# One fixed order of 966 operations exchanged for another, in a kernel of a state-space convolution and a gated MLP

## The chip, the core and the metric

The kernel runs on one core of a Trainium2 chip. The core has five engines with queues of their own: TensorE (PE in the profile; PEld is its weight load), VectorE (DVE), ScalarE (ACT), GpSimd (POOL) and SyncE (SP), which here only issues DMAs. An engine works off its queue in order. The metric is the device time of one launch in microseconds (us), lower is better.

## The reference

The input `u` (1 x 2048 x 512) is normalised along its last axis. The result is the sum of the input, a diagonal state-space convolution (S4) of the normalised rows, and a gated MLP (512 to 1792 and back) of them. Cut to what is computed:

```python
xn = layernorm(x)
# S4: kernel K from 128 modes for each of the 512 channels, then a causal convolution by FFT
dt = exp(log_dt)[:, None]
P = exp((dt * A)[:, :, None] * arange(2048)[None, None, :])
K = einsum("dn,dnl,dn->dl", C, P, dt * B).real
y = irfft(rfft(pad(xn)) * rfft(pad(K)))[:L] + xn * Dskip
# gated MLP
h = (sigmoid(xn @ w_gate) * (xn @ w_up)) @ w_down
return x + y + h
```

## The kernel before

The kernel builds a list of 966 operations with `_Plan.add`. Each has an engine, the operations that it depends on, and the buffers that it takes and gives back. The number of an operation in this list is its entry number below. `_Plan.run` goes through the hand-fixed list `ORDER` and emits the operations in exactly that order. Since an engine works off its queue in order, `ORDER` fixes the queue of each of the five engines. It also decides which buffer of a pool an operation gets: `run` takes the one that has been free longest. The framework puts a semaphore wait wherever an operation needs the result of another engine, or a buffer that another engine still reads. The plan's own costs play no part once `ORDER` is given.

The stages overlap. They are, in rough order of time:

- **Head, to about 16 us.** The first rows of x are loaded and normalised, TensorE is kept busy by warm-up products (L521), and the first gate products run.
- **Gated MLP.** The 2048 rows are four groups of 512. For each group there are 14 gate products (`fg`, L1036) and 14 up products (`fu`, L1060), each of four 128x128 by 512 matmuls. ScalarE takes the sigmoid (L1048, or L1051 for two at once), the up product is either copied by ScalarE (`feu`, L1072) or read from PSUM by VectorE, and VectorE multiplies (`fpd`, L1076). Four down products (`fd`, L1105, 14 matmuls each) end a group.
- **Kernel of the convolution.** ScalarE and VectorE build powers of the modes (L662 to L677, then L735 to L795 in four blocks), TensorE sums over the modes (L820).
- **Forward transform.** `fx2` (L694) transforms pairs of 128 rows, ScalarE or VectorE evicts them, and 16 stores write them to `z_scr` in HBM. All 16 must have landed before the first reload from it.
- **Units.** Twice eight units of half the channels each: a reload from `z_scr`, products `fm` (L882), an eviction, a swap of partition quarters (by DMA `big<-big` in the first half, by VectorE in the second), products with a table `c_E` (`fk`, L904), two VectorE multiplications (L909, L913), products back (`fv`, L926), an eviction and a store to `v_scr`.
- **Tail.** `reload()` reads `v_scr` back in three parts (entries 843 to 846, 847 to 850, 851 to 854), and the last products (`s2_mm`, L985) add the convolution to the MLP's results, beside the down products of the last group. Sums go out by DMA.

Products use different tile modes of TensorE: the large ones the whole array, `fm` and `fv` quarters of it, and others again halves or strips.

PSUM is 8 banks: two pairs (pool `s`) and four single banks (pool `gu`), so a product must wait until an earlier result has been read out of its bank.

Nearly all DMAs are issued by SP, in its order, some by ACT and POOL. A DMA that waits for data holds up all those behind it in SP's queue.

Of the kernel before, what the change touches and what calls it, by code (L numbers as in the profile page):

```python
# [178 lines left out]
def _consts():  # L179
# [20 lines left out]
ON_DVE = (88, 91, 106, 108, 123, 124, 125, 139, 140, 186, 196, 197, 200, 201, 203,)  # L200
ON_ACT = (2,)
ORDER = [
# [43 lines left out]

class _Op:
    __slots__ = ("alt", "tab", "eng", "cost", "fn", "prio", "acq", "rel", "dma", "left", "users", "ready", "start", "done", "seq", "mode")
# [946 lines left out]
```

## Time and profile before

| | |
|---|---|
| time of three runs | 218.53, 219.88, 219.86 us (median 219.86) |
| span of the profiled execution, first to last instruction | 217.6 us |
| TensorE busy | 209.0 us (96%), 1876 matmuls |
| VectorE busy | 193.8 us (89%) |
| ScalarE busy | 179.5 us (83%) |
| granted TensorE clock | 1.000 |
| moved by DMA | 42.80 MB |

The profile is of one execution. The page gives its span alone; the times of the runs are those of whole executions, and their median is 2.3 us above the span. A TensorE that counts as busy may still be in the pipeline of its matmuls, so its idle time is read from what it waited for. The helper that issues DMAs is one line (L421) and so is the copy by ScalarE (L287); they are told apart by the tiles that they write and read.

### The profile page before, as it was taken

To read this page: it belongs to the slowest core of one execution; us is meant where nothing else is said; L and a number is where in the kernel's file an instruction comes from. 1 tells how busy PE (TensorE), PEld (TensorE's weight loads), DVE (VectorE), ACT (ScalarE), POOL (GpSimd) and SP (SyncE) were. 2 spreads that over 40 slices of the span, in tenths; PEclk is the share of its full clock that TensorE was granted. 3 is DMA by queue.
4 is the path that set the end of the run, shared out by engine and by line. 5 is a ranking of instruction groups with operands and counts; after the bars stand their busy time and mean duration, and the time that the engine had idled before them with its cause. 6 is when DMAs were issued, how large, how long until landed. Compare 5 with 4: busy or idle time off the path is not lost.

```text
span 217.6 us, 4946 instructions
## 1 busy us (share of the span) xinstructions
PE 209.0 (96%) x1876; PEld 104.0 (48%) x1876; DVE 193.8 (89%) x438; ACT 179.5 (83%) x286; POOL 18.8 (9%) x40
## 2 busy tenths in 40 slices
PE   7979999999999999989999999999999999999894
PEld 2435444444444454435455565445546556544463
DVE  3989999999999999999999999999999999970433
ACT  3799999999999999869989999976897999960111
POOL 1410202002100020012000002010800000000000
PEclk9999999999999999999999999999999999999999
DMA  6999936001463689865697679929959969984974
GB/s 186 316 369 390 299 116 146 0 3 48 145 156 97 233 249 156 264 143 105 166 271 202 183 224 209 239 79 216 216 116 252 282 188 263 267 245 139 269 256 166
DMA packets 51530, 42.80 MB, mean 197 GB/s; under 512 B 16434, under 2 KB 43571, under 8 KB 51507
## 3 DMA queue, kind: packets, MB, share of 16 engines
q1 hardware_dynamic: 50338, 40.60, 63.8%
q0 software_dynamic: 864, 1.57, 5.5%
q10 hardware_dynamic: 304, 0.33, 0.6%
q8 instruction: 14, 0.23, 0.4%
q14 instruction: 10, 0.07, 0.1%
HBM read 25.97 MB, written 12.85 MB: 178 GB/s over the span
## 4 chain that ended last, share of the span: by engine, by line
PE 64%; DMA 17%; ACT 8%; SPq 7%; issue 2%; DVE 0%; ACTq 0%
PE bank L1060 18%; PE bank L1036 16%; PE bank L1105 10%; PE pair L904 7%; SPq L421 7%; DMA wu_sb<-in_B_w_up_dram 5%; PE pair L926 4%; ACT big L287 4%; DMA z_scr<-big 3%; DMA big<-big 3%; DMA big<-z_scr 2%; DMA v_scr<-big 2%; PE pair L882 2%; PE pair L820 2%; ACT us_sb L1072 2%
## 5 line engine op out<-in xcount | busy, mean ns | idle before, releaser
L287 ACT ACTIVATE big<-pair 128x1024 bf16<-128x1024 f32 x64 | 66.2, 1060 | 4.9 <-PE pair L926 1.5
L1060 PE MATMUL bank<-xnT,wu_sb 128*128 128x512 bf16 x224 | 54.5, 380 | 0.5 <-DMA wu_sb<-in_B_w_up_dram 0.4
L1036 PE MATMUL bank<-xnT,wg_sb 128*128 128x512 bf16 (+1 forms) x220 | 50.7, 368 | 1.9 <-DMA wg_sb<-in_B_w_gate_dram 1.8
L1105 PE MATMUL bank<-wd_sb,hT_sb 128*128 128x512 bf16 (+1 forms) x238 | 50.4, 367 | 0.0
L1036 PEld LDWEIGHTS <-wg_sb 128*128 128x128 bf16 x236 | 22.2, 98 | 26.9 <-issue 2.5
L1105 PEld LDWEIGHTS <-hT_sb 128*128 128x128 bf16 x238 | 22.6, 98 | 25.2 <-issue 1.9
L1060 PEld LDWEIGHTS <-wu_sb 128*128 128x128 bf16 x224 | 20.6, 98 | 25.2 <-issue 3.0
L1048 ACT ACTIVATE hT_sb<-bank 128x512 bf16<-128x512 f32 x52 | 30.9, 636 | 1.2 <-PE bank L1036 1.1
L735 DVE TENSOR_TENSOR big<-big 128x1024 bf16<-128x1024 bf16 (+4 forms) x40 | 26.8, 670 | 0.3 <-ACT big L287 0.2
L736 DVE TENSOR_TENSOR big<-big 128x1024 bf16<-128x1024 bf16 (+4 forms) x40 | 26.7, 667 | 0.0
L1072 ACT ACTIVATE us_sb<-bank 128x512 bf16<-128x512 f32 x40 | 25.9, 648 | 0.3
L909 DVE TENSOR_TENSOR big<-big 128x2048 bf16<-128x2048 bf16 x16 | 19.5, 1218 | 0.6 <-PE pair L926 0.3
L904 PE MATMUL pair<-big 128*128 128x256 bf16 x160 | 19.8, 273 | 0.0
L789 ACT ACTIVATE sq_sb<-big 128x256 bf16<-128x256 bf16 (+2 forms) x20 | 13.8, 691 | 5.1 <-DVE big L741 4.9
L904 PEld LDWEIGHTS <-big 128*128 128x128 bf16 x160 | 15.4, 98 | 4.9 <-issue 1.0
L1076 DVE TENSOR_TENSOR hT_sb<-hT_sb,us_sb 128x512 bf16<-128x512 bf16 x40 | 16.5, 418 | 0.4 <-ACT us_sb L1072 0.3
L740 DVE TENSOR_TENSOR big<-big 128x512 bf16<-128x512 bf16 (+4 forms) x40 | 16.5, 414 | 0.1
L741 DVE TENSOR_TENSOR big<-big 128x512 bf16<-128x512 bf16 (+4 forms) x40 | 16.5, 413 | 0.0
L1007 ACT ACTIVATE big<-pair 128x1024 bf16<-128x1024 f32 x3 | 3.1, 1023 | 15.2 <-PE pair L985 12.4
L895 DVE COPY big<-big 32x1024 bf16<-32x1024 bf16 x32 | 13.4, 419 | 0.6
L1011 DVE TENSOR_TENSOR big<-pair,glu_sb 128x1024 bf16<-128x1024 f32 x2 | 2.5, 1226 | 11.7 <-PE pair L985 8.1
L541 DVE BATCH_NORM_STATS2 stats<-big 128x6 f32<-128x512 bf16 x15 | 9.8, 682 | 3.4 <-DMA big<-in_A_u_dram 3.4
(104 smaller groups left out, 244.3 us busy)
## 6 DMA issues: line engine op xcount, KB each, us to landing
big<-c_E SPq DMA_DIRECT2D x16, 320.0 KB, 3.9
z_scr<-big SPq DMA_DIRECT2D x16, 256.0 KB, 2.9
big<-z_scr SPq DMA_DIRECT2D x16, 256.0 KB, 4.9
v_scr<-big SPq DMA_DIRECT2D x16, 256.0 KB, 3.1
big<-in_A_u_dram SPq DMA_DIRECT2D x4, 512.0 KB, 8.2
big<-big SPq DMA_DIRECT2D x32, 64.0 KB, 3.6
wu_sb<-in_B_w_up_dram SPq DMA_DIRECT2D x2, 896.0 KB, 10.7
wd_sb<-in_B_w_down_dram SPq DMA_DIRECT2D x1, 1792.0 KB, 15.1
```

Source lines behind the costliest of these rows:

```text
L287: nc.scalar.activation(out=get(out), in_=get(in_), func=ACT.Identity)
L735: V.tensor_tensor(out=wide(outp), in0=wide(lo), in1=mre, op=ALU.mult)
L736: V.tensor_tensor(out=wide(tb()), in0=wide(lo), in1=mim, op=ALU.mult)
L740: V.tensor_tensor(out=outp[:, :, 0], in0=outp[:, :, 0], in1=tb()[:, :, 1], op=opr)
L741: V.tensor_tensor(out=outp[:, :, 1], in0=outp[:, :, 1], in1=tb()[:, :, 0], op=opi)
L904: T.matmul(two(sk)[:, o:o + DW], es()[:, g, kt, :], kTv[p][:, :, kt, :], start=kt in (0, NKT - 1), stop=kt >= NKT - 2)
L909: V.tensor_tensor(out=pp().rearrange("p q h m -> p (q h) m"), in0=xx().rearrange("p q h m -> p (q h) m"), in1=kb()[:, 0:2 * DW].unsqueeze( ...
L1036: T.matmul(bank(sl, k % 2)[:, c0:c1], w[:, kt, k * 128:(k + 1) * 128], xnT[:, grp, kt, c0:c1], start=(kt == 0), stop=(kt == KT - 1))
L1048: S.activation(out=hT_sb[:, hs.idx, k % 2, :], in_=bank(sl), func=ACT.Sigmoid)
L1060: T.matmul(bank(sl), wu_sb[:, kt, k * 128:(k + 1) * 128], xnT[:, grp, kt, :], start=(kt == 0), stop=(kt == KT - 1))
L1072: S.activation(out=us_sb[:, us.idx, :], in_=bank(sl), func=ACT.Identity)
L1105: T.matmul(bank(po)[:, 0:c[1] - c[0]], hT_sb[:, hts[k // 2].idx, k % 2, jj * 128:(jj + 1) * 128], wd_sb[:, k, c[0]:c[1]], start=first and ...
```

## The change

Only the list `ORDER` changes. It holds the same 966 entries, so no operation, buffer, engine or size differs. The first 58 are in the same place; of the rest most move, by 7 places of the list in the median and by 433 at most. Of the 221 entries on TensorE 151 change their place in its queue, of VectorE's 284 it is 203, of ScalarE's 286 it is 230, of SP's 156 it is 119, and of POOL's 19 it is 14. Those that matter most stand below, with their places in the queue of their engine (counted from 0; an entry of ACT that only passes a dependency on counts too):

| entry | what it is | queue | place before | place after |
|---|---|---|---|---|
| 625, 628 | gate products 4 and 5, group 0 | PE | 24, 31 | 12, 20 |
| 658 | gate product 11, group 0 | PE | 23 | 22 |
| 645 | up product 8, group 0 | PE | 20 | 23 |
| 670 | up product 13, group 0 | PE | 33 | 24 |
| 660 | up product 11, group 0 | PE | 22 | 25 |
| 661 | ScalarE's copy of it | ACT | 23 | 22 |
| 105, 107 | normalisation of rows 4 and 6 (L548) | ACT | 29, 28 | 18, 21 |
| 100 | row statistics of row 7 | DVE | 27 | 24 |
| 109 | store of normalised rows of group 1 | SP | 16 | 16 |
| 110 | transposing reload of them | SP | 18 | 17 |
| 16 | load of the down weights | SP | 15 | 18 |
| 673 | first down product | PE | 46 | 46 |
| 158 | eviction of the last forward transform | ACT | 130 | 130 |
| 773, 818 | gate products 2 and 11, group 2 | PE | 90, 91 | 95, 107 |
| 813, 793, 783 | gate products 10, 6, 4, group 2 | PE | 94, 96, 107 | 83, 90, 92 |
| 396, 471 | first two `fm` of the units | PE | 93, 92 | 93, 94 |
| 462 | load of `c_E` for unit 2 | SP | 52 | 65 |
| 463 | its product `fk` | PE | 121 | 121 |
| 400 | a swap of unit 1 | SP | 55 | 64 |
| 512 | first reload from `z_scr`, second half | SP | 90 | 91 |
| 513 | its product `fm` | PE | 143 | 143 |
| 374 | bias sum on the kernel's second half (L841) | DVE | 243 | 241 |
| 677, 837 | accumulating DMAs of x | POOL | 8, 14 | 17, 18 |
| 23 | a warm-up matmul | PE | 200 | 220 |
| 535 | last store to `v_scr` | SP | 140 | 139 |
| 847, 850 | reloads of the second part, 384 KB each | SP | 139, 141 | 141, 140 |
| 851, 848 | reloads of the third and second part | SP | 142, 144 | 142, 143 |
| 601 | copy of a correction row (L957) | ACT | 279 | 281 |
| 852, 854 | reloads issued by ScalarE | ACT | 281, 280 | 279, 280 |
| 859, 855 | last products of row pairs 1 and 0 | PE | 207, 205 | 204, 205 |
| 862, 865 | last products of pairs 2 and 3 | PE | 211, 210 | 209, 210 |
| 954 | third down product of group 3 | PE | 209 | 211 |
| 845 | reload of the first part | SP | 145 | 148 |

The diff is the list itself, cut here to the first lines and the last; the first two lines of each are the same entries.

```diff
 ORDER = [
-    0, 1, 2, 14, 28, 38, 26, 29, 27, 3, 30, 39, 49, 32, 31, 40, 33, 41, 35, 18, 34, 4, 42, 43, 50, 24, 10, 44, 19,
-    51, 36, 45, 46, 11, 20, 52, 25, 5, 7, 37, 6, 53, 9, 47, 21, 48, 98, 96, 54, 643, 94, 663, 668, 55, 12, 644, 664,
-    97, 57, 56, 58, 653, 634, 60, 614, 654, 637, 615, 61, 100, 62, 101, 602, 603, 616, 604, 669, 13, 63, 608, 59,
-    648, 645, 196, 609, 660, 649, 95, 64, 65, 99, 658, 115, 610, 638, 625, 111, 646, 620, 647, 117, 113, 103, 232,
...
-    899, 377, 567, 526, 553, 906, 945, 554, 509, 568, 527, 907, 555, 569, 583, 911, 510, 900, 909, 529, 556, 910,
-    904, 547, 570, 530, 531, 893, 843, 844, 557, 511, 913, 532, 571, 912, 558, 933, 914, 894, 946, 533, 905, 934,
-    559, 923, 847, 534, 23, 895, 924, 915, 535, 935, 850, 858, 600, 925, 601, 947, 851, 854, 950, 852, 853, 855,
-    948, 856, 859, 848, 845, 949, 951, 860, 952, 954, 865, 862, 861, 958, 857, 866, 849, 953, 867, 863, 955, 959,
-    956, 864, 962, 872, 869, 868, 963, 870, 957, 871, 960, 873, 874, 875, 961, 964, 965]
+    0, 1, 2, 14, 28, 38, 26, 29, 27, 3, 30, 39, 49, 32, 31, 40, 33, 41, 35, 18, 34, 4, 42, 43, 50, 24, 10, 44, 19, 51,
+    36, 45, 46, 11, 20, 52, 25, 5, 7, 37, 6, 53, 9, 47, 21, 48, 98, 96, 54, 643, 94, 663, 668, 55, 12, 644, 664, 97,
+    653, 625, 100, 57, 101, 634, 56, 99, 614, 602, 603, 95, 102, 8, 615, 58, 654, 15, 60, 61, 62, 669, 22, 59, 637,
+    628, 604, 103, 648, 63, 64, 616, 13, 65, 658, 649, 104, 196, 106, 108, 645, 105, 670, 204, 646, 659, 660, 647,
...
+    837, 568, 843, 526, 554, 527, 906, 509, 907, 376, 846, 904, 569, 547, 510, 555, 511, 844, 911, 905, 945, 529, 570,
+    933, 556, 912, 530, 893, 531, 557, 571, 934, 913, 558, 532, 910, 533, 914, 559, 894, 923, 534, 935, 895, 924, 535,
+    858, 915, 600, 850, 847, 925, 851, 947, 950, 852, 854, 601, 859, 855, 848, 948, 958, 853, 860, 951, 849, 856, 862,
+    861, 857, 865, 845, 949, 954, 866, 952, 955, 959, 863, 867, 872, 869, 953, 960, 956, 864, 873, 868, 957, 962, 961,
+    870, 23, 963, 964, 874, 871, 875, 965]
```

67 rows, old and new, of the table ORDER are left out of this document.

## The prediction

> **What bounds the kernel now.** First the page's busy times, then each engine's busy time in stretches of the span (stretch, its length, then busy us and instruction count of PE, PEld, DVE, ACT and POOL, then granted clock, DMA share, GB/s).
>
> ```profile
> span 217.6 us, 4946 instructions
> PE 209.0 (96%) x1876; PEld 104.0 (48%) x1876; DVE 193.8 (89%) x438; ACT 179.5 (83%) x286; POOL 18.8 (9%) x40
> ...
> 12.00:30.00 18.00, 17.08 (x91) 8.78 (x92) 16.93 (x40) 17.70 (x31) 1.34 (x3) 1.00 0.87 301
> 75.00:88.00 13.00, 12.88 (x200) 6.24 (x193) 13.00 (x37) 13.00 (x25) 1.44 (x3) 1.00 0.93 198
> 88.00:98.00 10.00, 9.32 (x50) 4.06 (x47) 9.97 (x23) 7.23 (x14) 0.87 (x1) 1.00 0.70 186
> 192.00:202.00 10.00, 9.47 (x59) 3.95 (x57) 2.44 (x5) 1.82 (x3) 0.00 (x0) 1.00 0.64 187
> ```
>
> TensorE is 96% busy, VectorE has next to no idle time before 192 us, and ScalarE none from 75 to 88. A new order does no less work; it can only save idle time. So the second view is what TensorE waited for (us in all, times, longest):
>
> ```profile
> PE bank L1036 <- DMA wg_sb<-in_B_w_gate_dram: 1.8, 1, 1.8
> ...
> PE pair L985 <- DMA big<-v_scr: 0.8, 1, 0.8
> PE pair L882 <- DMA big<-z_scr: 0.7, 1, 0.7
> PE bank L1060 <- DMA wu_sb<-in_B_w_up_dram: 0.4, 1, 0.4
> ```
>
> The 1.8 lies in the untouched head. That leaves 0.4 + 0.7 + 0.8 = 1.9 us, under 1% of the span, and 0.1 in the stretch from 75 to 88. A gain of over 1% (2.2 us; 1% is also about what a measurement of this kernel can tell from no change) needs all of it. Losses have no such bound: whatever TensorE waits for anew adds to the span. The third view, the chain that ended last (start, us, what), shows the two reloads behind the last two waits:
>
> ```profile
> 88.51 1.02 ACT big L287
> ...
> 92.49 5.05 DMA big<-z_scr
> 97.59 0.63 PE pair L882 x8
> ...
> 194.31 4.82 DMA v_scr<-big
> 199.21 3.05 DMA big<-v_scr
> 202.30 0.52 PE pair L985 x6
> ...
> 214.51 0.42 DVE big L1125
> ```
>
> From 202.30 to 214.5 the chain is TensorE's own work; the 3.1 us behind it, the last sum and store, do not change.
>
> **Part 1, 12 to 98 us.** The new order puts products 625, 628 and 658 ahead of entry 645, the up product that waited 0.4 for its weights. That wait goes. A product of four matmuls takes 0.86, one that follows or precedes another tile mode 0.97:
>
> ```profile
> 22.79 0.86 PE bank L1060 x4
> ...
> 161.84 0.97 PE bank L1036 x4
> ```
>
> But entry 660, the up product 11 of the first row here, falls back. Ahead of it come four products (625, 628, 658, 670) and one warm-up matmul (0.2, a quarter of 0.86), and two half products (608, 609; 0.4 each) go behind: 3.4 + 0.2 - 0.9 - the 0.4 of the wait = 2.3 later. It ended at 23.65 and will end near 26.0. ScalarE's copy of it, entry 661 (the 25.33 row), moves only one place:
>
> ```profile
> 23.07 0.60 ACT L1048 ACTIVATE hT_sb<-bank 128x512 bf16<-128x512 f32 x1
> 23.55 1.04 ACT L1051 ACTIVATE hT_sb<-pair 128x1024 bf16<-128x1024 f32 x1
> 24.55 0.45 ACT L287 ACTIVATE big<-big 128x256 bf16<-128x256 bf16 x1
> 25.33 0.63 ACT L1072 ACTIVATE us_sb<-bank 128x512 bf16<-128x512 f32 x1
> 27.71 1.57 ACT L548 ACTIVATE big<-big,ln_nb_f,ln_ri_f 128x512 bf16<-128x512 bf16 x2
> ```
>
> Of what stood ahead of it, the first three rows (0.48, 0.90 and 0.31 to the next start) go behind it, and the two of the last row (1.45) come ahead. ScalarE is there at 25.1 and stands still for 0.9, with every later copy and sigmoid queued behind it. It has little idle time up to 88 us to win that back, and some 0.2 more work comes ahead of the last z eviction (the 88.51 row). I let the z store and the z reload behind it slip by 1.1: the reload lands at 98.6, not 97.5.
>
> TensorE meets that with more work ahead of its first z products (L882): gate products 813, 793 and 783 in place of 773 and 818, one product more. It is there at 97.59 - 0.7 - 0.4 + 0.86 = 97.35, does the z product whose load was first (0.3, half of the 0.63), waits until 98.6 and is through at 98.9. Before, it was through at 98.2 with 0.86 less done: **-0.1 us**. The ends: with no slip -0.4 - 0.7 = -1.1; each us of slip above 1.2 costs one.
>
> **Part 2, 98 to 192 us.** No wait of TensorE stands in the list for this stretch, so a load that comes too late can only lose. I compare a load's new place in SP's queue with the time at which that place was issued before, and add the page's median time to landing:
>
> ```profile
> 117.17 0.34 SPq L421 DMA_DIRECT2D big<-c_E  x1
> 134.57 3.56 SPq L421 DMA_DIRECT2D big<-z_scr  x2
> ...
> 120.66 1.25 PE L904 MATMUL pair<-big 128*128 128x256 bf16 x10
> 142.30 0.63 PE L882 MATMUL pair<-big,m 64*64 64x512 bf16 x8
> ```
>
> ```profile
> big<-c_E SPq DMA_DIRECT2D x16, 320.0 KB, 3.9
> ...
> big<-z_scr SPq DMA_DIRECT2D x16, 256.0 KB, 4.9
> v_scr<-big SPq DMA_DIRECT2D x16, 256.0 KB, 3.1
> ...
> wd_sb<-in_B_w_down_dram SPq DMA_DIRECT2D x1, 1792.0 KB, 15.1
> big<-v_scr SPq DMA_DIRECT2D x4, 384.0 KB, 5.0
> ```
>
> Entry 462 (a c_E load) goes back 13 places, to the one issued at 117.17: it lands at 121.1, and entry 463 wants it at 120.7: **+0.4** (0 to 0.5). Entry 512 (the first z load of the second half) goes from the first to the second DMA of the 134.57 row: at the latest 134.57 + 3.56 - 0.4 = 137.7, landing at 142.6; its product is the second half of the 142.30 row, at 142.5. The longest landing time on the other scratch tensor is
>
> ```profile
> DMA to landing us min/median/max: 2.4/4.6/6.0
> ```
>
> and with 6.0 it is 1.2 late. I take **+0.3**, nearer to the median (0 to 1.2). The swap load 400 goes back nine places, to one that by the same count lands about when VectorE wants it: 0. The bias sum 374 moves ahead of VectorE work and waits for the same load as before; that work is then done behind it: 0. One more change of tile mode costs 0.97 - 0.86 = **+0.1**. Two accumulating POOL DMAs (677, 837) move 9 and 4 places back and still stand tens of us ahead of their readers: 0.
>
> **Part 3, the tail.**
>
> ```profile
> 192.21 0.60 SPq L421 DMA_DIRECT2D big<-v_scr  x1
> 194.31 0.36 SPq L421 DMA_DIRECT2D v_scr<-big  x1
> 195.05 5.98 SPq L421 DMA_DIRECT2D big<-v_scr  x4
> ```
>
> The last warm-up matmul (23) goes behind everything: **-0.2**. TensorE came to the reloaded products at 202.30 - 0.8 = 201.5; with -0.1 + 0.4 + 0.3 + 0.1 - 0.2 = +0.5 it is there at 202.0. The reload itself: entry 847 (the first row, 384 KB) is now issued behind the last store (535, the second row) and no longer ahead of it. I give that store the median 3.1 instead of 4.82. Issued 0.7 later than before, it lands at 198.1, and its reload (3.05) at 201.2, ahead of TensorE. So the tail starts at 202.0: **0.3 gained**. The ends: 0.8 + 0.2 + part 1's 1.1 gained if nothing waits, and 0.7 lost if the store still takes 4.8.
>
> [...]
>
> Behind that start entries 862 and 865 now stand ahead of product 954 (3.1 us, a third of the 42.32 row below). Their load 848 is issued 0.6 behind 851, at 198.7, and with 5.0 lands at 203.7; it is wanted an estimated 2.1 into the tail (four reloaded groups of about 0.5, as the 202.30 row), at 204.1: 0 (up to 1.1). ScalarE's row copy 601 goes behind two DMA issues that wait for the store, and is done before the products that need it: 0. Load 845 goes behind two output stores and lands about when it is used: 0 (up to 1).
>
> Sum: **-0.3 us** on the profiled 217.6. The runs shown have their median 2.3 above that span, so 219.86 - 0.3 = **219.6 us**.
>
> **The rivals.** (a) All waits go: ScalarE doesn't slip and the last store is early, -0.4 - 0.7 - 0.8 - 0.2 - 0.1 = -2.2: 217.6. For it: VectorE's 1.1 us of idle time between 12 and 30 us is filled too, by entry 100. Against it: ScalarE's full stretches. (b) Slower, by one load: the down weights (16) move three places back in SP's queue, behind the transposing load.
>
> ```profile
> 29.30 0.40 SPq L421 DMA_DIRECT2D x_scr<-big  x1
> ...
> 32.27 2.17 SPq L580 DMA_TRANSPOSE xnT<-x_scr  x1
> ...
> 42.32 9.23 PE L1105 MATMUL bank<-wd_sb,hT_sb 128*128 128x512 bf16 x42
> ```
>
> From the x store to the end of the transposing issue are 5.1 us. If the store goes at 25.4 (the L548 that it needs come some 4 us earlier), the weights are issued at 30.5 and, with the 15.1 of before, land at 45.6, 3.3 after their use: TensorE waits, then ScalarE behind it, with no cover: 219.6 + 3.3 = 222.9. It decides from a landing time of 11.8 us on. Against it: before, the load queued behind three other large ones. (c) Slower, ScalarE's slip: its in-order copies wait for products put back between 30 and 88 us. A slip of 4 in place of 1.1 is +2.9: 222.5. (d) The tail gives its gain back, by 848 or 845 late: +1.1, 220.7.
>
> **How the numbers follow.** Chances: the forecast 0.38, (a) 0.22, (b) 0.16, (c) 0.17, (d) 0.07. Faster by over 1% is (a), 0.22; slower by over 1% is (b) and (c), 0.33; within 1% is the rest, 0.45. The forecast's own range, by the bounds of parts 2 and 3, is 218.4 to 221.5. The range that should hold 8 in 10 takes in (a) to just under it and (b) to just past it: 217.2 to 223.2.
>
> **What would show it.** Right: no TensorE wait on wu_sb; one wait of 0.5 to 1.2 on z_scr near 98; ScalarE idle for 0.9 ahead of an L1072 near 26; the last v_scr store landing in 2.5 to 3.5; L985 starting its tail without a wait near 202. Wrong: TensorE waiting on wd_sb at 42 (b); the z reload landing past 100 (c); L985 waiting in the middle of the tail (d); no wait near 98 (a).

## The result, and the profile after

The changed kernel takes 230.53 us (median of 4 runs, 229.73 to 232.84) beside 219.56 for the kernel before on the same chip: ratio 1.0549, 95% interval 1.0474 to 1.0624. The prediction was 219.6, within 217.2 to 223.2: it was wrong by 11 us. Times below are medians of all runs, and ratios leave out the runs more than 1.5% above the fastest of the same kernel, because with some of the kernels the mean granted clock is 1.00 in one run and 0.98 in the next. Each ratio is to the kernel before on the same chip, where its median was 218.2 to 219.1 us.

The profiled run has its span 10.3 us longer. The page's head, TensorE's row of slices and its clock:

```profile
span 227.9 us, 4919 instructions
PE 210.8 (92%) x1848; PEld 105.0 (46%) x1876; DVE 194.5 (85%) x438; ACT 179.4 (79%) x286; POOL 37.3 (16%) x40
PE   7899999999999999999999999996995699999694
PEclk9999999999999999999999999999999589999999
```

TensorE's digits drop at three places, a 6 some 70% of the way through, a 5 and a 6 behind it, and a 6 near the end; and the granted clock drops once, at the second. TensorE's list of waits names them (us in total, times, longest):

```profile
PE pair L903 <- DMA big<-c_E: 4.3, 1, 4.3
PE pair L984 <- DMA big<-v_scr: 2.5, 1, 2.5
PE pair L819 <- ACT big L286: 1.9, 1, 1.9
```

(Lines are one lower than in the kernel before.) The same work in TensorE's timeline, start and duration, first of the kernel before, then of the changed one: the burst f_k (entries 367 and 369), a product with a c_E load (541), a pair of down products (947, 950), the second pair of reloaded products:

```profile
154.44 1.75 PE L820 MATMUL pair<-big 128*32 128x82 bf16 x128
172.00 1.27 PE L904 MATMUL pair<-big 128*128 128x256 bf16 x10
195.03 6.22 PE L1105 MATMUL bank<-wd_sb,hT_sb 128*128 128x512 bf16 x28
202.30 0.30 PE L985 MATMUL pair<-big 128*64 128x256 bf16 x2 [0.83 <-DMA big<-v_scr]
```

```profile
155.71 0.80 PE L819 MATMUL pair<-big 128*32 128x82 bf16 x64
158.38 0.80 PE L819 MATMUL pair<-big 128*32 128x82 bf16 x64 [1.86 <-ACT big L286]
178.46 2.32 PE L903 MATMUL pair<-big 128*128 128x256 bf16 x10 [4.27 <-DMA big<-c_E]
203.93 6.22 PE L1104 MATMUL bank<-wd_sb,hT_sb 128*128 128x512 bf16 x28
212.88 0.30 PE L984 MATMUL pair<-big 128*64 128x256 bf16 x2 [2.50 <-DMA big<-v_scr]
```

So the 10.3 us add up: 155.71 - 154.44 = 1.3 up to 155; 0.9 more up to the c_E product less its own wait (178.46 - 4.27 - 172.00 = 2.2); 4.3 for the c_E load; 203.93 - 195.03 - 6.46 = 2.4 behind it; 10.58 - 8.90 = 1.7 at the tail; 0.3 won back to the end. One product, 888 (about 1 us), stands ahead of the burst in the new order and behind it in the old one. So about 1 of the first 1.3 is work done earlier, and the 0.9 is the wait of 1.9 less that product.

The 2.4 go to the clock: from the c_E product to the down products TensorE does the same work in both kernels, but for one warm-up matmul of 0.2, and in this stretch of the changed one it has no wait over 0.2. The windows (the number before the last two is the granted clock):

```profile
174.00:178.00 4.00, 0.19 (x8) 0.00 (x0) 3.92 (x8) 1.09 (x2) 0.00 (x0) 0.94 0.95 253
178.00:185.00 7.00, 6.38 (x39) 2.71 (x41) 2.10 (x3) 2.45 (x3) 0.00 (x0) 0.55 0.65 173
185.00:204.00 19.00, 18.73 (x183) 10.13 (x186) 16.65 (x33) 16.69 (x22) 0.00 (x0) 1.00 0.74 217
```

TensorE stood still for 4.3 us, and the mean clock of the 7 us behind it was 0.55.

Why was the c_E load late? GpSimd's timeline has the cause:

```profile
167.20 0.65 POOL L842 COPY hold<-big 1x1 bf16<-1x1 bf16 x1 [10.23 <-DVE big L840]
167.80 1.51 POOL L1141 DMA_DIRECT2D glu_sb<-in_A_u_dram  x2
168.90 1.30 POOL L1141 DMA_DIRECT2D big<-in_A_u_dram  x1
```

The copy 375 waits until 167.2, and the three accumulating transfers 762, 677 and 837 (each adds 256 KB of x to a tile) now stand behind it; in the old order they went out at 98, 80 and 145. The transfers between 169 and 177 by queue (packets, MB, share; then issues, KB, us to landing), and those of the kernel before between 166 and 172:

```profile
q0 software_dynamic: 431, 0.79, 60.8%
q1 hardware_dynamic: 1269, 0.92, 38.0%
...
big<-c_E SPq DMA_DIRECT2D x2, 320.0 KB, 7.9
```

```profile
q1 hardware_dynamic: 3438, 1.57, 97.5%
...
big<-c_E SPq DMA_DIRECT2D x3, 320.0 KB, 4.9
```

GpSimd's queue (q0) took 61% of the transfer engines' time just where SP's loads are due. SP also issued the load 540 later, first the row of the kernel before, then that of the changed one (540 and 504):

```profile
167.18 0.64 SPq L421 DMA_DIRECT2D big<-c_E  x1
170.63 1.12 SPq L420 DMA_DIRECT2D big<-c_E  x2
```

It landed 4.4 us after its issue before the change and 7.8 after it. With 4.4 it would have landed at 175.0, and TensorE wanted it at 178.46 - 4.27 = 174.2. So an estimated 0.8 of the wait is the later issue and 3.4 the slower landing.

The other two waits stand in the chain that ended last as late transfers, a v store (499) and the last store and reload (535, 851):

```profile
151.71 5.57 DMA v_scr<-big
...
203.43 2.38 DMA v_scr<-big
206.21 6.63 DMA big<-v_scr
```

### The profile page after: what moved, and what is told of

It reads as the page before. It is cut to its first block, busy times and chain, and to the rows that moved or that the text cites. A ratio compares the mean times of both kernels' runs of the same rounds, so it can differ in the third digit from the quotient of the medians.

```text
span 227.9 us, 4919 instructions
## 1 busy us (share of the span) xinstructions
PE 210.8 (92%) x1848; PEld 105.0 (46%) x1876; DVE 194.5 (85%) x438; ACT 179.4 (79%) x286; POOL 37.3 (16%) x40
## 4 chain that ended last, share of the span: by engine, by line
PE 35%; DVE 24%; DMA 17%; ACT 12%; SPq 4%; issue 3%; POOL 3%; ACTq 0%; DVEq 0%; POOLq 0%
PE bank L1104 11%; PE bank L1059 6%; ACT big L286 5%; PE bank L1035 5%; PE pair L903 5%; SPq L420 4%; DMA v_scr<-big 3%; PE pair L925 3%; DMA big<-c_E 3%; DVE stats L540 3%; DMA k_scr<-kq_sb 3%; DVE hT_sb L1075 3%; DMA big<-v_scr 3%; DMA big<-k_scr 3%; DVE big L608 2%
## 5 line engine op out<-in xcount | busy, mean ns | idle before, releaser
L286 ACT ACTIVATE big<-pair 128x1024 bf16<-128x1024 f32 x64 | 65.2, 1043 | 16.9 <-PE pair L903 8.3
L1059 PE MATMUL bank<-xnT,wu_sb 128*128 128x512 bf16 x213 | 53.7, 379 | 1.4 <-ACT us_sb L1071 0.4
L1071 ACT ACTIVATE us_sb<-bank 128x512 bf16<-128x512 f32 x40 | 24.5, 626 | 0.8 <-PE bank L1035 0.5
L903 PE MATMUL pair<-big 128*128 128x256 bf16 x160 | 20.8, 282 | 4.3 <-DMA big<-c_E 4.3
L903 PEld LDWEIGHTS <-big 128*128 128x128 bf16 x160 | 15.9, 100 | 9.9 <-DMA big<-c_E 4.5
L842 POOL COPY hold<-big 1x1 bf16<-1x1 bf16 x2 | 16.6, 8279 | 20.0 <-DVE big L840 20.0
L739 DVE TENSOR_TENSOR big<-big 128x512 bf16<-128x512 bf16 (+4 forms) x40 | 16.8, 420 | 0.1
L740 DVE TENSOR_TENSOR big<-big 128x512 bf16<-128x512 bf16 (+4 forms) x40 | 16.7, 419 | 0.0
L1006 ACT ACTIVATE big<-pair 128x1024 bf16<-128x1024 f32 x3 | 3.1, 1025 | 13.3 <-PE pair L984 13.3
L925 PE MATMUL pair<-big 64*64 64x512 bf16 (+1 forms) x256 | 13.3, 338 | 0.0
```

The lines of the kernel that those rows point to most:

```text
L286: nc.scalar.activation(out=get(out), in_=get(in_), func=ACT.Identity)
L903: T.matmul(two(sk)[:, o:o + DW], es()[:, g, kt, :], kTv[p][:, :, kt, :], start=kt in (0, NKT - 1), stop=kt >= NKT - 2)
L925: T.matmul(two(sv)[o:o + 64, DW * (2 * g + y):2 * DW * (g + 1)], mab[b:b + 64, 2 * u + g, q, :], pq()[b:b + 64, q, ch] if y else pp()[b:b ...
L1059: T.matmul(bank(sl), wu_sb[:, kt, k * 128:(k + 1) * 128], xnT[:, grp, kt, :], start=(kt == 0), stop=(kt == KT - 1))
L1071: S.activation(out=us_sb[:, us.idx, :], in_=bank(sl), func=ACT.Identity)
```

## The experiments

Theories: **P**, the three accumulating transfers make the c_E load late; **V**, the v store 499 is late in SP's queue and holds ScalarE's copy; **R**, reload 847 behind the last store makes the tail late. Rivals: **S**, SP's queue alone makes the load late; or the new order costs something of its own. Lists of numbers are entries in a queue's order. The waits and landing times of each kernel come from one profiled run.

**1. GpSimd's old queue.**

The whole queue goes back; places 2 to 6 are cut from the list here.

```diff
 GpSimd, places 8 to 18
-682 290 757 280 336 378 842 375 762 677 837
+677 757 762 290 336 682 837 842 378 280 375
```

> The new order with GpSimd's queue alone put back into the old order, so that the accumulating transfers 762, 677 and 837 no longer stand behind the copy 375, which waits until 167.2. Theory P (these three 256 KB transfers run beside the c_E load 540 at 169 to 177 and make it land 7.8 us after issue): 540 lands within 5 us of its issue, TensorE's wait of 4.3 on it falls to 1 or less, the granted clock stays at 1.00 between 176 and 186, and the time goes from 230.5 to about 224 (223 to 225); the wait of 1.9 at 157 stays. Rival S (540 is late because SP's queue stood behind the v store 454 until 168.3): 540 still lands after 177, the wait and the clock of 0.50 stay, and the time is 229.5 to 231.

Ten runs, 219.9 to 228.5: three with the clock at 1.00 took 219.9 to 222.3 (ratio 1.0114, 1.0055 to 1.0172), seven at 0.977 to 0.992 took 225.8 to 228.5. The c_E load is gone from TensorE's waits; instead:

```profile
PE pair L820 <- issue: 3.3, 1, 3.3
PE pair L985 <- DMA big<-v_scr: 2.5, 1, 2.5
```

TensorE comes to the product 3.4 us later here than in the changed kernel, so the missing wait alone proves little; the landing time of the load decides:

```profile
big<-c_E SPq DMA_DIRECT2D x1, 320.0 KB, 4.4
```

P holds for the load. Where the load goes out within 3 us of the first of the three transfers, it takes 7.8 (the changed kernel), 6.0 (number 7) and, by the end of TensorE's wait, 8 (number 2); in all other kernels with its landing on record, 3.0 to 5.2. The clock now drops at a wait of 3.3 in f_k that the profile puts down to nothing ("issue"). That was new.

**2. The v store.**

```diff
 SP, places 94 to 106
+499
 445 443 469 326 431 444 430 446 588 429 524 428
-499
```

> The new order with one entry moved: the v store 499 goes from place 106 of SP's queue to place 94, ahead of the swap load 445. Theory V (the late store 499 holds ScalarE's copy 423 until 157.3, and that holds the f_k product 369): TensorE's wait of 1.9 on a pair buffer at 157 goes and ScalarE waits for no v store there. With theory P of the accumulating transfers the c_E load 540 is still held by them, so the time falls by 0 to 1.5 only, to about 229.7. Rival S (the load 540 is late since the slip of 3 us carries on through copy 453 and store 454 into SP's queue): the load goes out 2 us earlier, lands before 175, the wait on it falls below 1.5 and the clock does not drop: about 223.5.

230.61 us, ratio 1.0595 (1.0508 to 1.0682). ScalarE waits for no v store any more; the c_E load stays late in TensorE's waits:

```profile
PE pair L904 <- DMA big<-c_E: 3.4, 1, 3.4
```

V and P hold, and S falls as the only cause: the load goes out 1.3 us earlier (169.32), and TensorE still waits 3.4 for it. The median does not fall. (The move also gives nine v copies another buffer.)

**3. The tail's reload.**

```diff
 SP, places 137 to 141
 571
+847
 559 535 850
-847
```

> The new order with one entry moved: the 384 KB reload 847 goes back ahead of the last v store 535 and of store 559, the place that it had before. Theory R (the last reload 851 took 6.6 us because 847 and 850 were both in flight ahead of it): the last store lands later (4 to 5 us instead of 2.4), 851 lands within 4 us of its issue, TensorE's wait of 2.5 at the tail falls to about 1.2, time 229.2 (228.7 to 229.8). Rival: store and reload trade one for the other and the wait stays at 2.5, time 230.5 within 0.4.

232.28 us, ratio 1.061 (1.052 to 1.070), and the wait for the reload is 3.2 long and not 1.2. The landing times of the last store and of reload 851:

```profile
v_scr<-big SPq DMA_DIRECT2D x1, 256.0 KB, 5.5
big<-v_scr SPq DMA_DIRECT2D x1, 128.0 KB, 3.2
```

The reload is as quick as R says, 3.2 in place of 6.6, but the store takes 5.5 in place of 2.4. The two trade, as the rival has it: 847 slows the transfer that stands behind it, and moving it alone wins nothing.

**4. The three together.**

> The three single edits together (GpSimd's old queue, v store 499 ahead of the swap load 445, reload 847 ahead of the last v store). If the three places are the whole loss, the time is back at 219.5 (218.8 to 220.3) and TensorE has no wait over 1.3 us behind 20 us. If the order as a whole costs something beside them (transfers, engines' queues), at least 221.5 is left.

227.4 us, ratio 1.0415 (1.0329 to 1.0501): the three places are not the whole loss, or not mended in this way. Behind the f_k wait, now 1.2, TensorE came to entry 600, ahead of the tail, at 195.01 beside 194.71 in the old kernel, so the first two places are mended. Then the waits:

```profile
PE pair L985 <- DMA big<-v_scr: 2.8, 1, 2.8
PE bank L985 <- DMA big<-v_scr: 1.7, 1, 1.7
```

**5. SP's tail.** Number 4, and SP's queue from place 121 on in the old order:

```diff
-598 595 552 439 564 528 946 377 583 523 843 376 846 547 511 844 571 847 559 ...
+439 376 598 564 523 552 846 528 595 377 583 547 843 844 511 571 946 559 847 ...
```

> The new order with GpSimd's old queue, the v store 499 ahead of the swap load 445, and SP's queue from place 121 on in the old order (the 512 KB reloads 846, 843, 844 ahead of the stores 547 and 511 and the load 946, reload 847 ahead of store 559); the other engines keep the new order. With the first two edits and reload 847 alone TensorE reached the tail only 0.3 behind the old kernel and then waited 2.8 and 1.7, with the clock at 0.50 for 6.8 us. Theory Q (the place of the large reloads in SP's queue makes those waits): both waits together fall to 1.3 or less, the clock stays at 1.00 up to 215, and the time is within 1% of the old kernel. Rival F (the new order of TensorE's own tail, product 954 ahead of the others, and the copies make them): at least 2.5 of the waits stay and the time is 3% or more above the old kernel.

225.8 us, 1.0264 (1.0204 to 1.0325). The tail's waits are down to 0.9 in all, with no drop of the clock there: the order of SP's tail was the cause, though this edit moves many entries and does not say which. Most of the rest is the wait in f_k, here in TensorE's timeline:

```profile
157.24 1.36 PE L820 MATMUL pair<-big 128*32 128x82 bf16 x121
162.07 0.33 PE L820 MATMUL pair<-big 128*32 128x82 bf16 x7 [3.47 <-issue]
```

A window of it: TensorE is idle for the first 1.2 us, and the clock is 0.50 for the whole of the 6.8.

```profile
160.90:167.70 6.80, 5.41 (x25) 1.67 (x27) 2.40 (x7) 3.96 (x6) 0.00 (x0) 0.50 0.31 75
```

**6. Only the 512 KB transfers of the tail.** Numbers 1 and 2, with 846 behind 564, 843 and 844 ahead of 547, 946 behind 571; 847 stays behind 535:

> The new order with GpSimd's old queue, v store 499 ahead of the swap load 445, and only the 512 KB transfers back near their old places in SP's queue: reload 846 seven places earlier, reload 843 and 844 ahead of stores 547 and 511, load 946 behind store 571. Reload 847 stays where the new order has it, behind the last v store 535. Theory Q with the 512 KB reloads as the cause: the store 571 lands within 3.5 us of its issue, the waits at the tail sum to 1.5 or less, time within 1.5% of the old kernel. Theory with 847 as the cause: the last reload 851 still needs 6 us or more, the waits sum to 2.3 or more, and the clock drops in the tail; 3% above the old kernel.

224.5 us (219.96 to 228.32; too far apart for a ratio). The tail waits once, for 2.2, not the 1.5 that I expected with the reloads as the only cause; reload 851 needs 6.3, and the clock drops in the tail, both as expected with 847 as the cause. In every kernel with 847 behind the store 535 and a landing on record, 851 took 6.3 to 6.8; with 847 ahead of it, 2.8 to 4.7. So 847 decides how late the last reload is; what the large reloads add is not separated from the rest of SP's tail.

**7 and 8. One queue alone.** The old order with GpSimd's new queue, and the old order with SP's new queue:

> The old order with GpSimd's queue alone in the new order, so that the accumulating transfers 762, 677 and 837 stand behind copy 375 (165.6 in the old kernel). Theory P (these three beside SP's loads are enough): the c_E load 540 lands after 174 instead of 171.6, TensorE waits 2 to 4 for it near 173, the clock drops to 0.50 in at least half of the runs, and the time is 3 to 9 us above the old kernel. Rival S (they harm only with SP's queue late): no wait over 1 near 173, time within 1%.

> The old order with SP's queue alone in the new order; GpSimd's transfers stand where they stood. Theory of three places: a wait of 1 to 3.5 near 156 behind the v store 499, 2 to 4 at the tail behind the large reloads, no wait over 1 for c_E load 540 near 173; the time 3 to 9 us above the old kernel, depending on whether the clock drops. Rival (the new places in SP's queue are bearable and it is TensorE's, ScalarE's and VectorE's new order that meets them badly): time within 1% of the old kernel.

GpSimd's queue alone: 222.02 us, 1.0156 (1.0105 to 1.0207), waits of 1.2 in all for c_E, less than the 2 to 4 expected, as SP's loads go out earlier there (540 at 166.4), and 1.8 at the tail in place of 0.8. SP's queue alone: 231.51 us, 1.059 (1.053 to 1.065), as much as the whole change and more than expected, by two of TensorE's waits and 6.8 us of half clock at the first:

```profile
PE pair L820 <- ACT big L287: 5.5, 1, 5.5
PE bank L1105 <- DMA wd_sb<-in_B_w_down_dram: 1.8, 1, 1.8
```

The first is V: ScalarE waits 6.5 for the store 499. The second is the prediction's rival (b), which in the changed kernel does not show: there TensorE comes to the down products at 40.94 and does not wait. The tail, with 1.4 of waits, is below the 2 to 4 expected. The parts do not add up: in the profiled runs an earlier wait leaves the later loads more time (number 1: TensorE is 3.4 us later at the c_E product and does not wait there). Nor is number 8 SP's queue alone: interleaved in this way, the list hands out 151 buffers differently, 115 of them PSUM banks.

**9 to 11. What is the wait in f_k?** In numbers 1 and 3 to 6 it stands at one place, behind 121 of the 128 matmuls, and ends 1.3 to 1.5 us after a packet of 16 KB on the instruction queue (q8) has landed. The packet in the kernel before (152.8 to 153.9) and in number 5 (159.6 to 160.7):

```profile
q8 instruction: 1, 0.02, 5.3%
```

```profile
q8 instruction: 1, 0.02, 5.4%
```

In the kernel before and in the changed one it goes out at TensorE's load 1241 and 1244, ahead of the burst; in number 5 only at load 1371, when TensorE has come to a stand. The kernel before has 14 such packets, on average 126 loads and as many matmuls apart (61 to 205 loads); its page has them as

```profile
q8 instruction: 14, 0.23, 0.4%
```

The stall lies 128 loads and 128 matmuls behind load 1243. In the kernel before TensorE goes through this stretch in 2.4 us, and through the others of the same length, counted from there, in 6 to 26. That the packets hold TensorE's code and that the stall waits for one of them is my reading; no trace shows what a packet holds. First I took SP's burst of loads for what delays the packet (theory I), and the engines' new order as innocent (theory D):

```diff
 SP, number 5, places 103 to 109
-588
 429
-524
 428
-516 584
 394
+584 588 516 524
```

> The kernel of the run before (new order, GpSimd's old queue, v store 499 ahead of 445, SP's old tail from place 121) with four loads moved: z load 584, c_E loads 588 and 516 and z load 524 go from places 103 to 108 of SP's queue to places 106 to 109, behind the v store 394, so that they are issued after 154 instead of 148 to 151. Theory I (TensorE's stall in the middle of the f_k product 369 near 156 is the fetch of its next 16 KB of instructions, which has to pass the burst of transfers issued at 142 to 154): the instruction packet goes out before 155.5, the stall at TensorE's load 1371 falls from 3.5 to 1.2 or less, no drop of the clock behind it, and the time is 219 to 222, within 1.5% of the old kernel. Rival W (369 waits for a pair buffer or for a store that the profile does not name): the stall stays at 1.2 to 4.5 and the clock drops in most runs.

225.71 us, 1.0302 (1.0233 to 1.0372). Theory I falls: the transfer engines were idle (share 0.00, the number before the last) at 154.0, when TensorE came to load 1243, and the packet went out only after 157.4:

```profile
152.20:155.40 3.20, 3.20 (x41) 1.53 (x40) 3.20 (x7) 2.90 (x5) 1.10 (x2) 1.00 0.00 0
```

TensorE's timeline in the same kernel:

```profile
159.89 0.26 PE L820 MATMUL pair<-big 128*32 128x82 bf16 x7 [2.72 <-issue]
```

The engines' new order with both queues old, from 80 us or from 122 us on:

> The new order of TensorE, VectorE and ScalarE; GpSimd's queue and SP's queue from place 32 on (about 80 us) in the old order. Theory D (the loss is wholly in the order of the two transfer queues): no wait over 1.3 near 156, 173 or at the tail, and the time is within 1% of the old kernel, 217 to 220.5. Rival E (the new order of the engines itself costs more than 1%): 2% or more above the old kernel with the same waits as with the new queues, or with new ones.

> As the kernel with the old queues, but SP's queue keeps the new order up to place 69 (about 122 us) and takes the old one from there. Theory D with the harm in the places from 74 on: the same time as with the old queue from place 32 on, within 1%. If the first 70 places of the new queue matter as well, 1 to 3% more, with the waits ahead of 125.

225.13 us, 1.0203 (1.0147 to 1.026), and 225.98, 1.0332 (1.0274 to 1.0391). Theory D falls: the engines' new order costs 2% with the old queues as well. The f_k wait is 3.9 and 3.7, and with the old queue from 80 us on TensorE also waits 3.1 for z loads.

**12 to 14. The accumulating transfer 842.** In numbers 1, 4 to 6 and 9 to 11 this transfer goes out 0.1 us behind load 1243, about where the packet goes out in the kernel before, and in some of them the packet goes out within about 0.5 us of its landing. Theory J takes it for what holds the packet:

```diff
 GpSimd, old order
 837
-842
 378 280
+842
 375
```

> The kernel with the old tail of SP's queue (new order, GpSimd's old queue, v store 499 ahead of 445, SP's old order from place 121) with one entry moved: the accumulating transfer 842 goes on GpSimd's queue from ahead of the memset 378 to behind the copy 280, so that it is issued after 157 instead of at 153 to 155. Theory J (TensorE's stall at its load 1371 is the fetch of its next 16 KB of instructions, held behind the accumulating transfer 842 that GpSimd issues within 0.2 us of the same moment): the instruction packet goes out within 2 us of load 1243, the stall at load 1371 falls from 3.7 to 0.6 or less, the clock stays at 1.00 up to 215, and the time is within 1% of the old kernel. Rival K (the fetch is late because of SP's transfers or of a reason in TensorE's own stream): the stall stays above 1.2 and the time 2.5% above.

> The kernel with the new order of TensorE, VectorE and ScalarE and the old queues of SP (from place 32 on) and GpSimd, with the accumulating transfer 842 moved behind the copy 280. Theory J: the stall of 3.9 at load 1371 goes, the time falls from 2% above the old kernel to within 1%. Rival K: stall and time stay.

> The new order with GpSimd's old queue alone, and in it the transfer 842 behind the copy 280; SP's queue is the new one throughout. Theories P and J together: no wait over 1 on the c_E load near 173, no instruction stall at load 1371; what stays is the wait of about 2 near 157 for ScalarE's copy behind the v store 499 and the waits of 2 to 4 at the tail, the time 2 to 5 us above the old kernel where the clock holds and up to 4 more where it drops in the tail. Rival: the stalls of 3.3 near 157 stay as with GpSimd's old queue alone, 226 to 228 in most runs.

On number 5: 223.25 us, 1.0234 (1.019 to 1.0278), stall 2.3 in place of 3.5. With the engines' order alone: 227.14 us, 1.036, stall 1.9. On number 1: 225.59 us, 1.0307, stall 1.7. The stall does not go, so theory J is at most a part of it.

**15 to 17. The copies ahead of it, and the first half.** Theory L: a product just ahead of load 1243 starts late, because copies 839 and 841 wait behind copy 434 in ScalarE's queue, and the packet goes out late with it. Its two tests on number 5 put product 433 ahead of 840 on TensorE, or copies 839 and 841 ahead of 434 on ScalarE. The third run has the new order for its first 460 entries and the old one behind:

> The kernel with the old tail of SP's queue (new order, GpSimd's old queue, v store 499 ahead of 445, SP's old order from place 121) with one entry moved on TensorE: the f_k-side product 433 goes back ahead of the down product 840, as in the old order. [...] Rival M (the fetch is late for what the transfer engines do at that time): the stall stays above 1.2.

> The kernel with the old tail of SP's queue, TensorE's order untouched, with two entries moved on ScalarE: copies 839 and 841 go ahead of copy 434, so that they no longer wait behind it for product 433. Theory L: 841 ends 1 us or more ahead of load 1243, the packet goes out before load 1243, the stall at load 1371 falls to 0.6 or less, time within 1%. Rival M: the stall stays above 1.2.

> The new order up to about 98 us (its first 460 entries) and the old order for the rest. The prediction's part 1 by itself: no wait on wu_sb at 21, a wait of 0.5 to 1.2 on z_scr near 98, TensorE 0.1 ahead at 98, time within 0.4% of the old kernel. If the whole loss lies behind 98 us, within 1%; if the first half costs something that the later stalls hide, 1 to 2% above.

223.17 us, 1.0226, stall 1.9; 225.9 us, 1.0346, stall 2.8: the stall is shorter in the first but stays above the 0.6 expected, and theory L falls. The first half: 225.01 us, 1.0196 (1.0142 to 1.025), and not the 0.4% of the prediction's part 1. There TensorE's order around f_k is the old one, and it stalls at the same load, now behind 125 matmuls, as one product of four stands behind the burst and not ahead of it:

```profile
157.31 1.70 PE L820 MATMUL pair<-big 128*32 128x82 bf16 x125
162.25 0.26 PE L820 MATMUL pair<-big 128*32 128x82 bf16 x3 [3.25 <-issue]
```

**18. 64 matmuls ahead.** Number 5 with its list untouched. The burst then lies 64 loads and 64 matmuls later in TensorE's stream, half of the 128 that lie between load 1243 and the stall:

```diff
                 T.matmul(bank(wsl), glu_sb[:, 0, 0:128], glu_sb[:, 0, :], start=True, stop=True)
+            for i in range(64 if prio == -7 else 0):
+                T.matmul(bank(wsl)[32 * (i % 4):32 * (i % 4) + 32, 0:82], glu_sb[:, 0, 0:32], glu_sb[:, 0, 0:82],
+                         start=True, stop=True, tile_position=(0, 32 * (i % 4)))
```

> The kernel with the old tail of SP's queue (new order, GpSimd's old queue, v store 499 ahead of 445, SP's old order from place 121), its list untouched, with 64 narrow matmuls (32 weight columns, 82 columns moved, on zeros) added to TensorE's last warm-up entry ahead of the first gate product, inside its wait of 1.2 to 1.8 for the gate weights at 11. [...] Theory N (what is left after the mends is the fetch of the block that the burst uses up in 3 us): TensorE has no stall over 0.9 between 150 and 170, the clock does not drop there, and the time falls from 223.7 to 227.3 to within 1.2% of the old kernel (217.5 to 221). Rival W (the product 369 waits for something else there): the stall of 2 to 4 near 158 stays.

221.65 us, 1.0117 (1.0046 to 1.0187), all five runs at a clock of 0.999 or 1.000, beside 225.8 for number 5. The burst runs through in its timeline:

```profile
157.35 1.41 PE L823 MATMUL pair<-big 128*32 128x82 bf16 x128
```

Theory N holds in what it says of the stall, which was 3.5, and of the ratio, which falls from 1.0264 to 1.0117. That the burst had used up the code at hand before the late packet was there stays my reading of it. What holds the packet back for up to 5 us in one kernel and not in another stays open: neither SP's loads, 842 nor the copies explain it alone. In the last 1.2% TensorE's list has 1.4 of waits for c_E loads and 1.3 at the tail, 0.5 more than before; no run tests them. No version beat the kernel before.

## Why the prediction was wrong, step by step

**Part 2, the accumulating transfers: the step that failed.** The prediction gave 677 and 837 a price of 0 because they "still stand tens of us ahead of their readers". That was so, and nobody waited for them. But it priced the reader and not the road: behind copy 375 these two and 762, which it does not mention, went out together at 168, on the transfer engines that SP's c_E load needed (61% of their time between 169 and 177). In place of 0, the wait there is 4.3, an estimated 3.4 of it by these transfers, and the half clock behind it costs 2.4: two thirds of the loss of the profiled run. Numbers 1 and 7 show the cause, with GpSimd's old queue in the new order and its new queue in the old one.

**Part 2, SP's places.** "I compare a load's new place in SP's queue with the time at which that place was issued before" was done for loads alone. The entry that cost was a store: 499, four places back, frees a buffer that ScalarE's next copy writes. ScalarE waited for it:

```profile
157.30 1.02 ACT L286 ACTIVATE big<-pair 128x1024 bf16<-128x1024 f32 x1 [2.27 <-DMA v_scr<-big]
```

A place, moreover, is not a fixed time: 445, ahead of it in both orders, went out at 144.2 and before at 145.9, and still 499 went out 2.0 later than before, at 151.7, since eleven issues of about 0.6 stand between the two and no longer five. Among these transfers it took 5.6 to land, and before 3.25. The loads that I did price (462, 512) did not make TensorE wait.

**Part 3, the tail.** The store was right: 2.4 to landing where I expected 2.5 to 3.5. The reload behind it was not: 6.6 in place of the 3.05 that I took over from before. In that row one 384 KB load (850) was issued between the store and 851, and now two are (850, 847): the sum went by a row that no longer applied. Number 3 adds that the store and the reload trade: 847 slows whichever of them stands behind it (851 takes 6.6 or 3.2, the store 5.5 or 2.4). What mended the tail was SP's whole order there (number 5).

**Part 1** came out near its number, and partly by luck. There was no wait for wu_sb, and TensorE was through the first z products at 98.9, as forecast. But it came to them at 98.1 and not at 97.35, and did not wait for the z reload at all, as in rival (a); and ScalarE's idle time ahead of copy 661 was 0.34 and not 0.9. With the new first half alone (number 17) TensorE did wait 1.1 there, until 99.5, where the kernel before waited until 97.6. (The term itself, 98.9 - 98.2 - 0.86, is -0.2 and not -0.1.)

**The rivals.** (b) was real and hidden (number 8). (c) had the form of what happened, in-order copies on ScalarE, but not the place or the cause. (d) had the tail's direction, but 848 and 845 were not what it waited for. None had the clock in it: each wait was priced at its own length, and a wait of 4.3 cost 6.7 here. That is why the range was too narrow on the slow side; it names no case in which a wait costs more than its own length.

## What to carry to other kernels

When an order of many queues is changed, price a moved transfer three times: for its reader, for the buffer that it frees, and for whatever it will run beside; a transfer that nobody waits for can still be the dearest one. Queue places are not times: ask what blocks the queue ahead, and what goes out in one burst when it opens. And in these runs every TensorE wait of 3.2 us or more came with half clock and so cost more than its length; of several waits the longest is to be found first.

## What the runs showed of the hardware

In the profiled runs TensorE's clock fell to 0.50 for 3.4 or 6.8 us at each of the ten waits of 3.2 to 5.5 us, during the wait or just behind it. Of the waits of 1.9 to 2.8 us eight came with such a drop (numbers 1, 3, 4, 6, 9 and 16, and two in 13), and six did not, the 2.5 at the changed kernel's tail and the 2.6 of number 14 among them. Below 3.2 the length alone does not decide.

TensorE stood still for 1.2 to 4.5 us in f_k in 14 of these kernels, with no semaphore, under the releaser "issue", in the middle of one burst of small matmuls. The kernel before goes through the same stretch of 128 loads and 128 matmuls in 2.4 us; its packet landed at 153.8, ahead of the burst at 154.4, in the profiled run. That it is TensorE's own code that is late is my reading, from two things: in numbers 1 and 3 to 6 the stall ends 1.3 to 1.5 us after a 16 KB packet on the instruction queue has landed, and with 64 matmuls more in an idle microsecond the burst of number 18 runs through in 1.41. Beside number 18, three of the nine runs of the kernel before took 221.2 to 226.4 at a clock of 0.977 to 0.992 and the others about 218; that they stalled there is likely but not shown.
